# A kernel with sessions of matmuls on one core: small work between them spaced by sessions

## The chip, the cores and the metric

The kernel runs on one core of one Trainium2 chip. The metric is the time of one execution on the device in microseconds (us), first instruction to last with what lies around them; lower is better.

## What is computed

Agent attention for 4 batches, then a feed-forward layer with a squared ReLU on all 49920 tokens:

```python
def _attn_ref(q, k, v, agents):          # q, k, v: 4 x 12480 x 128; agents: 4 x 49 x 128
    scale = 1.0 / np.sqrt(q.shape[-1])
    def sm(a, b):
        s = scale * (a @ b.transpose(0, 2, 1))
        s = s - s.max(-1, keepdims=True)
        e = np.exp(s)
        return e / (e.sum(-1, keepdims=True) + 1e-09)
    agent_v = sm(agents, k) @ v          # 49 x 128 for each batch
    return sm(q, agents) @ agent_v

def _moe_ref(x, w_in, w_out):            # 128 -> 2048 -> 128
    h = np.maximum(x @ w_in, 0.0)
    return h * h @ w_out
```

The product of `agent_v` and `w_in` is formed once for each batch (the *table*, 49 x 2048), so a token needs its 49 softmax weights times the table (h), ReLU, square, and the product with `w_out`. Numbers are split into a high and a low part, so that products of short floats keep the precision of the long ones.

## The kernel before

Tokens go through in 52 *groups* of 960 (13 to a batch). A group has two halves of 480 tokens, a half has 8 *slots* of 256 hidden columns, and a half's slots go through in three *sessions* of 3, 3 and 2 slots (`SIZES`). A group's six sessions are called A1, A2, A3 (first half) and B1, B2, B3 here; A3 and B3 are the short ones. Session s does, in the loop at the end of the kernel:

- `first`: TensorE makes h of session s (`h<-w` with the weights w and the table's high part, then `h<-x` with the 19 rows of x that hold the rest), and ScalarE takes the ReLU (`r<-h`), slot by slot;
- `copied_out`: VectorE copies a finished half out of its PSUM bank (`ob<-o`; there is one such bank, `ps_o`);
- `squares`: ScalarE squares r (`r<-r`);
- `halved`: VectorE splits session s-1 into `g_hi` and `g_lo`;
- `second`: TensorE multiplies session s-2 by `w_out`: all `o<-g_hi`, then all `o<-g_lo` (LAG is 2).

On TensorE's queue a session is thus its h, then the products of the session two before it. Small work is put in between by Python generators, and one PSUM bank (`psa`, `ps_a` with bufs=1) takes all of its matmuls in turn: each must wait until the last one's result has been read.

- `queries` (named "ahead") makes one group's softmax weights, a group before they are used: the load of qt; its scores (`psa<-ag,qt`, 32 small matmuls); on VectorE m (maximum) and e; on ScalarE the exponential; on VectorE z, its reciprocal and `e<-e,z`; on ScalarE the cast to `pp`, on VectorE the low part `pp<-e,pp`; then for each half four transposes (`psa<-identr,pp`), ScalarE's `w<-psa` (w0, w1) and DMAs from w to w and to x. The transposes always stand behind the `o` products of B1 and B2 (a yield of "turn" marks them).
- `background(b)` (named "todo") makes the next batch's table: 13 blocks of keys (`psa<-ag,kt`, ScalarE's copy `s<-psa`, VectorE's `mx`), the maxima (`m1`, `dg`, `mb`), 13 blocks of values (`psa<-d,vt`, VectorE's `av`, then the next `d<-s,mb`), the sums (`rl`), and four products `psa<-win,avT`, each read by ScalarE's `aw_hi` and VectorE's `aw_lo`. It runs during three of the four batches; the last 13 groups have none.

A generator yields either nothing (its next step is taken by `between`, one for a slot, while "todo" is behind its goal) or a number of slots (its next step stands in `first`, at most one in a session, "ahead" before "todo"). What is issued through `queued` keeps this written order on its engine; other small instructions are placed by the scheduler, which models the engines. Weights w and x of half j are read by `h` of the next group's A1 (w0, x0) and B1 (w1, x1).

Of the kernel before, what the change touches and what calls it, by code (L numbers as in the profile page):

```python
# [17 lines left out]
P = 128  # L18
# [7 lines left out]
WIDEST = max(SIZES)  # L26
# [7 lines left out]
PRE = 10  # L34
RAW = 4
CT = 32
SPREAD = 0.88
BEGIN = 4
FIRST = 7

# [2 lines left out]
def agent_attention_relu2(ctx: ExitStack, tc: tile.TileContext, qT, kT, v, agT, w_in, w_out, outT):  # L43
    nc = tc.nc
    C, NTOK = qT.shape
    _, B, NA = agT.shape
    N = NTOK // B
    FF = w_in.shape[1]
# [3 lines left out]
    NK = len(blocks)  # L52
    K2 = 2 * NA
# [16 lines left out]
    class Ordered:  # L70
        def __init__(self, eng, always=False):
            self.eng, self.always = eng, always
# [6 lines left out]

    pe, act, dve, pool, sync = (Ordered(e) for e in (nc.tensor, nc.scalar, nc.vector, nc.gpsimd, nc.sync))  # L80

    fixed = Ordered(nc.scalar, True)

    def spare():
        return pool if alone[0] else dve
# [103 lines left out]
    def scores(b, i, kt):  # L189
        st = state.setdefault(b, {"s": []})  # L190
        _, rows, nt = blocks[i]
        yield 3
        sv = bank()[:rows, : nt * NA].rearrange("p (t a) -> p t a", a=NA)
        for t in range(nt):
            tiled(sv[:, t, :], kt[:, t * rows : (t + 1) * rows], ag[:, b, :])
        s = sp.tile([P, 512], F32, name="s")[:, : NT * NA].rearrange("p (t a) -> p t a", a=NA)
        st["s"].append(s)
        if i == 0:
            st["mx"] = small.tile([P, NT, NA], F32, name="mx")
        s, mx = (x[:rows, :nt, :] for x in (s, st["mx"]))  # L200
        fixed.copy(s, sv)
        if i == 0:
            dve.tensor_copy(mx, s)
        else:
            dve.tensor_max(mx, mx, s)

    def maxima(b):
        st = state[b]
        m1 = small.tile([P, NA], F32, name="m1")
        dve.reduce_max(m1, st["mx"].rearrange("p t a -> p a t"), axis=AX.X)  # L210
        yield
        pt = bank()
        pe.transpose(pt[:NA, :P], m1, ident)
        yield
        m2 = small.tile([NA, 1], F32, name="m2")
        dve.reduce_max(m2, pt[:NA, :P], axis=AX.X)
        dg = small.tile([NA, NA], F32, name="dg")
        dve.tensor_scalar_mul(dg, ident[:NA, :NA], m2)
        yield
        pb = bank()  # L220
        pe.matmul(pb[:, :NA], ones[:NA, :], dg, start=True, stop=True)
        yield
        st["mb"] = small.tile([P, NA], F32, name="mb")
        dve.tensor_copy(st["mb"], pb[:, :NA])

# [13 lines left out]
    def whole_sums(b):  # L239
        st = state[b]  # L240
        e1 = small.tile([P, 2, NA], F32, name="e1")
        dve.reduce_sum(e1[:, 0, :], st["mx"].rearrange("p t a -> p a t"), axis=AX.X)
        dve.tensor_copy(e1[:, 1, :], e1[:, 0, :])
        yield
        av = st["avT"] = small.tile([C, K2], F32, name="avT")
        dve.tensor_copy(av[:, :NA], st["av"])
        dve.tensor_copy(av[:, NA:], av[:, :NA])
        pz = bank()
        pe.matmul(pz[:K2, :1], e1.rearrange("p h a -> p (h a)"), ones[:, :1], start=True, stop=True)
        rl = st["rl"] = small.tile([K2, 1], F32, name="rl")  # L250
        dve.tensor_scalar_add(rl, pz[:K2, :1], 1e-9)
        dve.reciprocal(rl, rl)
# [20 lines left out]
    def tables(b):  # L273
        st = state[b]
        rl, av = st["rl"], st["avT"]
        hi = st["hi"] = aw.tile([P, FF], F32R, name="aw_hi")
        ex = st["lo"] = aw.tile([P, NCH // NQ, P], F32R, name="aw_ex")
        for n in range(FF // 512):
            yield
            cs = slice(n * 512, (n + 1) * 512)  # L280
            pw = bank()
            pe.matmul(pw[:K2, :], av, win[:, cs], start=True, stop=True)
            yield
            fixed.activation(hi[:K2, cs], pw[:K2, :], AF.Copy, scale=rl)
            lo = aw.tile([P, 512], F32R, name="aw_lo", bufs=3)[:NA, :]
            dve.scalar_tensor_tensor(  # L286
                out=lo, in0=pw[:NA, :], scalar=rl[:NA, :], in1=hi[:NA, cs].bitcast(F32),
                op0=ALU.mult, op1=ALU.subtract,
            )
            yield  # L290
            sync.dma_start(hi[K2:, cs].bitcast(F32), lo[:SP, :].bitcast(F32))
            for t in range(NQ):
                sync.dma_start(ex[t * 32 : t * 32 + NL, n, :].bitcast(F32), lo[SP:, t * P : (t + 1) * P].bitcast(F32))


    weights = {}
    slot = [0]

    def queries(g):
        b = g // NB  # L300
        qt = qp.tile([C, BLK], F32, name="qt", bufs=1)
        sync.dma_start(qt, qT[:, g * BLK : (g + 1) * BLK])
        yield 3
        ps = ps_a.tile([P, 512], F32, name="psa")
        sv = ps[:TP, : NT * NA].rearrange("p (t a) -> p t a", a=NA)
        for t in range(NT):
            tiled(sv[:, t, :], qt[:, t * TP : (t + 1) * TP], ag[:, b, :])
        if alone[0]:
            yield
        m = qp.tile([TP, NT, 1], F32, name="m", bufs=1)  # L310
        dve.reduce_max(m, sv, axis=AX.X)  # L311
        e = qp.tile([TP, NT, NA], F32, name="e", bufs=1)
        dve.tensor_sub(e, sv, m.broadcast_to([TP, NT, NA]))  # L313
        yield
        if not alone[0]:
            yield
        act.activation(e, e, AF.Exp, scale=scale)  # L317
        yield
        z = qp.tile([TP, NT, 1], F32, name="z", bufs=1)
        dve.reduce_sum(z, e, axis=AX.X)  # L320
        dve.tensor_scalar_add(z, z, 1e-9)
        dve.reciprocal(z, z)
        spare().tensor_mul(e, e, z.broadcast_to([TP, NT, NA]))  # L323
        yield
        pp = qp.tile([TP, NT, K2], F32R, name="pp", bufs=1)
        yield from halves(pp, e, NA, spare())
        weights[g] = []
        for j in range(2):
            yield "turn"
            pt = ps_a.tile([P, 512], F32, name="psa")  # L330
            for t in range(NT // 2):
                queued(
                    nc.tensor.matmul, nc.tensor, pt[:K2, t * TP : (t + 1) * TP], pp[:, j * (NT // 2) + t, :], identr, start=True, stop=True
                )
            w = qp.tile([P, G], F32R, name=f"w{j}", bufs=2)
            x = qp.tile([P, G], F32R, name=f"x{j}", bufs=2)
            fixed.copy(w[:K2, :], pt[:K2, :G])
            weights[g].append((w, x))
            yield
            sync.dma_start(w[K2:, :].bitcast(F32), w[:SP, :].bitcast(F32))  # L340
            for t in range(NQ):
                sync.dma_start(x[t * 32 : t * 32 + NL, :].bitcast(F32), w[SP:NA, :].bitcast(F32))
# [4 lines left out]
    SLOTS = 2 * NP  # L347
# [4 lines left out]
    def first(k, m):  # L352

        g, i = divmod(k, SLOTS)
        j, c = divmod(i, NP)
        b = g // NB
        w, x = weights[g][j]
        hs = [ps_h.tile([P, 2, 512], F32, name="h") for _ in range(m)]
        outs = [(2 * c + n, hs[n // 2][:, n % 2, :G]) for n in range(2 * m)]
        for n, out in outs:  # L360
            cs = slice(n * P, (n + 1) * P)
            queued(nc.tensor.matmul, nc.tensor, out, state[b]["hi"][:, cs], w, start=True, stop=False)

        with tc.high_priority():
            for n, out in outs:
                t = n % NQ
                rows = slice(t * 32, t * 32 + NL)
                queued(nc.tensor.matmul, nc.tensor, out, state[b]["lo"][rows, n // NQ, :], x[rows, :], start=False, stop=True)
        r = ffn.tile([P, WIDEST, 2, G], F32, name="r", bufs=RB)
        for x, h in enumerate(hs):  # L370
            queued(nc.scalar.activation, nc.scalar, r[:, x, :, :], h[:, :, :G], AF.Relu)
        for name in ("ahead", "todo"):
            if type(stands.get(name)) is int and k >= stands[name] and done[name] < goal[name]:
                move(name, k)
                break
        return r
# [65 lines left out]
        yield from whole_sums(b)  # L442
        yield from tables(b)

    STEPS = 2 + 2 * NK + 5 + 3 * NK + 1 + 3 * (FF // 512)

    def step(gen):

# [65 lines left out]
    turn = {}  # L514
# [179 lines left out]
    def between(k):  # L694
# [10 lines left out]
            following[0] = queries(g + 2)  # L705
            step(following[0])
        if c == 0 and 0 < g < B * NB - 1:
            gens["ahead"], stands["ahead"] = following[0], k + 1
        if stands["ahead"] is None and k > 0:
            move("ahead", k)  # L710

# [6 lines left out]
    made, split = {}, {}  # L718
    for s in range(len(sessions) + LAG):
        k, m = sessions[s] if s < len(sessions) else (total, 0)  # L720
        if s == LAG:
            behind = [chain[eng] for eng in (nc.tensor, nc.sync, nc.scalar, nc.vector, nc.gpsimd)]
        if m:
# [12 lines left out]
            halved(*sessions[s - 1], made.pop(s - 1), s <= LAG)  # L736
        if s >= LAG:
            second(*sessions[s - LAG])
            if stands.get("ahead") == "turn":
                move("ahead", slot[0])  # L740
        for x in range(1, m):
            between(k + x)
# [36 lines left out]
```

## Time and profile before

| | before |
|---|---|
| median of 3 runs (lowest to highest) | 2105.43 us (2100.71 to 2107.95) |
| the profiled execution: its time | 2101.62 us |
| its span, first to last instruction | 2099.6 us |
| mean granted TensorE clock | 0.969 |
| busy: TensorE, VectorE, ScalarE | 93 %, 78 %, 78 % |

In the profile PE is TensorE's matmuls, PEld its weight loads, DVE VectorE, ACT ScalarE, SP the queue of DMA issues. Nearly every row of PE, DVE and ACT carries line L64, the helper `queued`, so rows are told apart by their tiles (`o<-g_hi,wo_lo`). A timeline row gives the start, the duration, the engine, the operation and its tiles, how many alike were merged, and in brackets how long the engine had stood idle and who ended that.

### The profile page before, as it was taken

Reading aid. Unit: us, or ns where it says so; the run is one execution under the profiler, and the core shown is the slowest. Engines: PE = TensorE matmul, PEld = TensorE weight load, DVE = VectorE, ACT = ScalarE, POOL = GpSimd, SP = SyncE. Lnnn points to the kernel's source line nnn. Section 1 sums busy time; section 2 is a strip of 40 time slices with the busy share of each in tenths; the row PEclk is TensorE's granted clock in tenths of the full one; section 3 lists DMA queues with packets and bytes.
Section 4 is the critical chain, followed back from the end, with each engine's and each line's share of the span. In section 5 each row is a group of like instructions: output and inputs, shape, how many; then the busy total and the mean of one; then the engine's idle time right before and its main releaser. Section 6 shows DMA issues by size and latency. Waiting matters only on the chain.

```text
span 2099.6 us, 39766 instructions
## 1 busy us (share of the span) xinstructions
PE 1959.2 (93%) x17181; PEld 1508.9 (72%) x17181; DVE 1640.4 (78%) x1371; ACT 1637.7 (78%) x1516; POOL 20.6 (1%) x24
## 2 busy tenths in 40 slices
PE   7899999998999999998989999999899899989989
PEld 4677777776777777776767777777677677767767
DVE  7778888887778888887767888888677767767866
ACT  5788878887778888887777888888777777777876
POOL 3000000000000000000000000000000000000000
PEclk9999999999999999999999999999999999989989
DMA  9222222211112212211112212121111011001100
GB/s 359 75 83 73 67 73 78 67 53 40 39 62 78 87 59 80 82 59 36 43 41 77 82 52 82 60 70 45 32 40 42 27 37 39 32 30 36 42 20 25
DMA packets 54818, 131.46 MB, mean 63 GB/s; under 512 B 6508, under 2 KB 34828, under 8 KB 54644
## 3 DMA queue, kind: packets, MB, share of 16 engines
q1 hardware_dynamic: 54644, 128.93, 18.6%
q8 instruction: 135, 2.21, 0.4%
q14 instruction: 39, 0.32, 0.0%
HBM read 80.97 MB, written 25.56 MB: 51 GB/s over the span
## 4 chain that ended last, share of the span: by engine, by line
PE 55%; ACT 18%; DVE 17%; issue 9%; DMA 1%; SPq 0%; POOL 0%; ACTq 0%; DVEq 0%; POOLq 0%
PE o L64 32%; PE h L64 18%; ACT r L64 17%; DVE g_hi L64 7%; DVE g_lo L64 5%; PE psa L64 4%; DVE ob L64 1%; DVE pp L231 1%; DVE m L311 1%; DVE z L320 0%; DVE t L64 0%; DVE e L323 0%; DMA ahead<-in_kT 0%; DVE mx L64 0%; DMA x<-w 0%
## 5 line engine op out<-in xcount | busy, mean ns | idle before, releaser
L64 ACT ACTIVATE r<-h 128x960 f32<-128x960 f32 x832 | 752.0, 973 | 290.5 <-PE h L64 287.5
L64 DVE TENSOR_TENSOR g_lo<-r,g_hi 128x2880 fp32r<-128x2880 f32 (+2 forms) x315 | 880.4, 2796 | 15.0 <-PE psa L64 0.9
L64 ACT ACTIVATE r<-r 128x2880 f32<-128x2880 f32 (+2 forms) x315 | 733.0, 2328 | 7.7
L64 DVE CAST g_hi<-r 128x2880 fp32r<-128x2880 f32 (+2 forms) x315 | 464.9, 1476 | 291.8 <-ACT r L64 282.7
L64 PE MATMUL o<-g_hi,wo_lo 128*128 128x480 f32 x1664 | 682.5, 410 | 7.1 <-DVE ob L64 6.9
L64 PE MATMUL o<-g_hi,wo_hi 128*128 128x480 f32 x1664 | 647.6, 389 | 0.0
L64 PE MATMUL h<-w,aw_hi 128*128 128x480 f32 x1664 | 426.2, 387 | 0.4 <-DVE aw_hi L64 0.4
L64 PE MATMUL o<-g_lo,wo_hi 128*128 128x480 f32 x1664 | 426.2, 388 | 0.0
L64 PEld LDWEIGHTS o<-g_hi,wo_lo 128*128 128x128 f32 x1664 | 322.2, 194 | 117.3 <-issue 44.7
L64 PEld LDWEIGHTS o<-g_lo,wo_hi 128*128 128x128 f32 x1664 | 322.5, 194 | 52.6 <-issue 1.5
L64 PEld LDWEIGHTS o<-g_hi,wo_hi 128*128 128x128 f32 x1664 | 323.5, 194 | 42.1 <-issue 0.7
L64 PEld LDWEIGHTS h<-w,aw_hi 128*128 128x128 f32 x1664 | 305.6, 189 | 47.6 <-issue 2.0
L64 PE MATMUL h<-x,aw_ex 19*128 19x480 f32 x1664 | 204.4, 467 | 2.3 <-DMA x<-w 2.3
L64 PEld LDWEIGHTS h<-x,aw_ex 19*128 19x128 f32 x1664 | 84.8, 188 | 110.9 <-issue 107.9
L64 DVE COPY ob<-o 128x480 f32<-128x480 f32 x104 | 67.6, 650 | 84.7 <-PE o L64 84.3
L64 PE MATMUL psa<-identr,pp 120*98 120x120 f32 x416 | 54.9, 256 | 72.8 <-DVE pp L231 62.5
L64 PEld LDWEIGHTS psa<-identr,pp 120*98 120x98 f32 x416 | 50.8, 173 | 98.7 <-DVE pp L231 55.5
L64 ACT CAST w<-psa 98x480 fp32r<-98x480 f32 x104 | 57.2, 550 | 50.0 <-PE psa L64 50.0
L64 PE MATMUL psa<-ag,qt 128*32 128x49 f32 (+1 forms) x3328 | 48.4, 213 | 26.2 <-DVE aw_lo L286 21.7
L64 PEld LDWEIGHTS psa<-ag,qt 128*32 128x32 f32 (+1 forms) x3328 | 41.1, 111 | 43.2 <-DVE aw_lo L286 24.2
L231 DVE TENSOR_TENSOR pp<-e,pp 120x392 fp32r<-120x392 f32 x51 | 28.8, 564 | 21.0 <-ACT pp L229 21.0
L317 ACT ACTIVATE e<-e 120x392 f32<-120x392 f32 x51 | 26.7, 524 | 22.4 <-DVE e L313 22.2
(138 smaller groups left out, 624.4 us busy)
## 6 DMA issues: line engine op xcount, KB each, us to landing
qt<-in_qT SPq DMA_DIRECT2D x52, 480.0 KB
out_T<-ob SPq DMA_DIRECT2D x104, 240.0 KB
kt<-in_kT SPq DMA_DIRECT2D x36, 512.0 KB
vt<-in_v SPq DMA_DIRECT2D x36, 512.0 KB
x<-w SPq DMA_DIRECT2D x416, 35.6 KB
ahead<-in_kT SPq DMA_DIRECT2D x12, 512.0 KB
ahead<-in_v SPq DMA_DIRECT2D x12, 512.0 KB
w<-w SPq DMA_DIRECT2D x104, 56.2 KB
```

Source lines behind the costliest of these rows:

```text
L64: ins = issue(*args, **kw)
L231: eng.tensor_sub(out[:, :, n : n + w], x, out[:, :, :w].bitcast(F32))
L311: dve.reduce_max(m, sv, axis=AX.X)
L317: act.activation(e, e, AF.Exp, scale=scale)
```

## The change

- `queries`: its steps begin at slot 0 of a group and not at slot 1. A block of transposes waits for `Turn`: the first for two sessions after the step that made pp's low part, the second for the next session's end. While one is due, "todo" takes its step in `first` only in a session of full width (`due`).
- `scores`, `maxima`, `whole_sums`: other spacing, and the transposes and products of the maxima and sums go in their written place on TensorE (`put`).
- `tables`: the product and its two readers are issued in one step, two slots apart.
- `SPREAD` 0.88 becomes 0.98: the background's goal reaches the whole of its steps later in the batch; `STEPS` counts the fewer steps.

```diff
-SPREAD = 0.88
+SPREAD = 0.98
...
-    fixed = Ordered(nc.scalar, True)
+    fixed, put = Ordered(nc.scalar, True), Ordered(nc.tensor, True)
...
     def scores(b, i, kt):
-        yield 3
+        yield 2
...
         dve.reduce_max(m1, st["mx"].rearrange("p t a -> p a t"), axis=AX.X)
-        yield
+        yield 2
         pt = bank()
-        pe.transpose(pt[:NA, :P], m1, ident)
-        yield
+        put.transpose(pt[:NA, :P], m1, ident)
...
-        yield
+        yield 3
         pb = bank()
-        pe.matmul(pb[:, :NA], ones[:NA, :], dg, start=True, stop=True)
-        yield
+        put.matmul(pb[:, :NA], ones[:NA, :], dg, start=True, stop=True)
...
         for n in range(FF // 512):
-            yield
+            yield 2
             cs = slice(n * 512, (n + 1) * 512)
             pw = bank()
-            pe.matmul(pw[:K2, :], av, win[:, cs], start=True, stop=True)
-            yield
+            put.matmul(pw[:K2, :], av, win[:, cs], start=True, stop=True)
             fixed.activation(hi[:K2, cs], pw[:K2, :], AF.Copy, scale=rl)
...
+    class Turn:
+        def __init__(self, wait):
+            self.session = session[0] + wait
+
+    def due():
+        at = stands.get("ahead")
+        return isinstance(at, Turn) and session[0] >= at.session
...
         for j in range(2):
-            yield "turn"
+            yield Turn(0 if j or slot[0] < SLOTS else 2)
...
         for name in ("ahead", "todo"):
-            if type(stands.get(name)) is int and k >= stands[name] and done[name] < goal[name]:
+            if (m == WIDEST or not due()) and type(stands.get(name)) is int and k >= stands[name] and done[name] < goal[name]:
...
-    STEPS = 2 + 2 * NK + 5 + 3 * NK + 1 + 3 * (FF // 512)
+    STEPS = 2 + 2 * NK + 5 + 3 * NK + 1 + 2 * (FF // 512)
...
-            gens["ahead"], stands["ahead"] = following[0], k + 1
+            gens["ahead"], stands["ahead"] = following[0], k
...
             second(*sessions[s - LAG])
-            if stands.get("ahead") == "turn":
+            if due():
                 move("ahead", slot[0])
```

The change moves instructions on every engine. VectorE in a group of the last batch, before, from z in A2 to the split of B1 (`r` is what ScalarE squared; 2880 is a session of three slots, 1920 of two):

```order
L320 TENSOR_REDUCE z<-e 120x8
L64 TENSOR_TENSOR g_lo<-r,g_hi 128x2880
L321 TENSOR_SCALAR z<-z 120x8
L64 CAST g_hi<-r 128x1920
L322 RECIPROCAL z<-z 120x8
L64 TENSOR_TENSOR g_lo<-r,g_hi 128x1920
L323 TENSOR_TENSOR e<-e,z 120x392
L64 CAST g_hi<-r 128x2880
L231 TENSOR_TENSOR pp<-e,pp 120x8x49
L64 TENSOR_TENSOR g_lo<-r,g_hi 128x2880
```

The same engine and work in the changed kernel, from the end of B3 of the group before to the split of A2:

```order
L319 TENSOR_TENSOR e<-psa,m 120x392
L64 CAST g_hi<-r 128x2880
L326 TENSOR_REDUCE z<-e 120x8
L64 TENSOR_TENSOR g_lo<-r,g_hi 128x2880
L327 TENSOR_SCALAR z<-z 120x8
L64 COPY ob<-o 128x480
L328 RECIPROCAL z<-z 120x8
L329 TENSOR_TENSOR e<-e,z 120x392
L64 CAST g_hi<-r 128x2880
L229 TENSOR_TENSOR pp<-e,pp 120x8x49
L64 TENSOR_TENSOR g_lo<-r,g_hi 128x2880
```

The low part of pp, which the transposes behind the products of B1 read, stood between the halves of the split of B1; now it stands in that of A2, two sessions earlier, and z has moved in front of `ob`, where m stood.

VectorE in the same place of a group with blocks of values behind it, in the changed kernel (A1):

```order
L64 CAST g_hi<-r 128x2880
L326 TENSOR_REDUCE z<-e 120x8
L64 TENSOR_TENSOR g_lo<-r,g_hi 128x2880
L327 TENSOR_SCALAR z<-z 120x8
L268 TENSOR_TENSOR av<-av,psa 128x49
L235 TENSOR_TENSOR d<-s,mb 128x392
L328 RECIPROCAL z<-z 120x8
L329 TENSOR_TENSOR e<-e,z 120x392
L64 COPY ob<-o 128x480
```

Here four small operations stand between `z<-z` and `ob` that stand behind it, or elsewhere, in the other groups.

ScalarE at the last product of a table, before:

```order
L64 ACTIVATE r<-h 128x960 x3
L64 ACTIVATE r<-r 128x2880
L64 ACTIVATE aw_hi<-psa,rl 98x512
L317 ACTIVATE e<-e 120x392
L229 CAST pp<-e 120x8x49
```

and in the changed kernel, at the last two:

```order
L64 ACTIVATE r<-h 128x960 x3
L64 ACTIVATE aw_hi<-psa,rl 98x512
L64 ACTIVATE r<-r 128x2880
L227 CAST pp<-e 120x8x49
L64 ACTIVATE r<-h 128x960 x2
L64 ACTIVATE aw_hi<-psa,rl 98x512
L64 ACTIVATE r<-r 128x1920
```

`aw_hi`, which reads the product out of the bank, has moved in front of the squares of the session that issues the product; before, it stood behind the squares of the session after it.

## Rows read from the trace of the kernel before

**Rows 1.** The page, part 1: busy us, share, instructions of each engine.

```profile
PE 1959.2 (93%) x17181; PEld 1508.9 (72%) x17181; DVE 1640.4 (78%) x1371; ACT 1637.7 (78%) x1516; POOL 20.6 (1%) x24
```

**Rows 2.** Waits of PE: who waited for whom, total us, times, longest us.

```profile
PE psa L64 <- DVE pp L231: 62.5, 32, 3.3
PE psa L64 <- DVE aw_lo L286: 21.7, 6, 6.6
PE psa L64 <- DVE av L270: 9.4, 12, 1.1
PE o L64 <- DVE ob L64: 6.9, 24, 0.6
```

**Rows 3.** Timeline of PE, last batch: the transposes behind B1's products.

```profile
1597.70 0.56 PE L64 MATMUL psa<-identr,pp 120*98 120x120 f32 x4 [3.27 <-DVE pp L231]
```

**Rows 4.** Windows: length; busy of PE, PEld, DVE, ACT, POOL; PEclk; DMA share, GB/s.

```profile
1010.92:1045.19 34.27, 33.98 (x233) 26.63 (x232) 26.82 (x18) 29.23 (x25) 0.00 (x0) 1.00 0.13 42
1010.92:1017.26 6.34, 6.34 (x36) 5.03 (x34) 3.45 (x3) 4.38 (x4) 0.00 (x0) 1.00 0.00 0
1017.26:1022.37 5.11, 5.11 (x31) 3.94 (x30) 4.04 (x2) 4.48 (x6) 0.00 (x0) 1.00 0.08 20
1588.19:1598.09 9.90, 6.63 (x35) 4.94 (x34) 7.98 (x9) 6.26 (x6) 0.00 (x0) 1.00 0.00 0
1598.09:1606.26 8.17, 8.17 (x30) 6.01 (x30) 2.81 (x2) 5.86 (x5) 0.00 (x0) 0.58 0.07 21
345.63:352.84 7.21, 6.57 (x36) 4.94 (x34) 6.11 (x10) 4.82 (x6) 0.00 (x0) 1.00 0.00 0
352.84:359.76 6.92, 6.21 (x95) 4.65 (x94) 5.39 (x5) 6.73 (x6) 0.00 (x0) 1.00 0.14 39
810.64:848.85 38.21, 36.94 (x425) 28.81 (x424) 32.28 (x31) 31.51 (x29) 0.00 (x0) 1.00 0.24 79
1536.00:1541.59 5.59, 5.59 (x90) 4.36 (x88) 4.22 (x2) 4.86 (x5) 0.00 (x0) 1.00 0.27 78
1492.92:1507.60 14.68, 8.12 (x89) 6.42 (x88) 8.64 (x10) 8.32 (x8) 0.00 (x0) 0.65 0.13 36
```

**Rows 5.** Timeline, last batch, A1 to A3: end of h, the split, ob, pp.

```profile
1572.25 0.70 PE L64 MATMUL h<-x,aw_ex 19*128 19x480 f32 x6
...
1578.17 1.66 DVE L64 CAST g_hi<-r 128x2880 fp32r<-128x2880 f32 x1 [4.11 <-ACT r L64]
...
1583.48 0.65 DVE L64 COPY ob<-o 128x480 f32<-128x480 f32 x1
...
1584.18 0.48 PE L64 MATMUL o<-g_hi,wo_lo 128*128 128x480 f32 x1 [0.24 <-DVE ob L64]
...
1597.08 0.56 DVE L231 TENSOR_TENSOR pp<-e,pp 120x392 fp32r<-120x392 f32 x1
```

**Rows 6.** Timeline of PE at the end of a batch: the table's last products.

```profile
1486.36 1.10 PE L282 MATMUL psa<-win,avT 128*98 128x512 f32 x2 [1.56 <-DVE aw_lo L286]
...
1501.59 1.53 PE L64 MATMUL psa<-ag,qt 128*32 128x49 f32 x64 [6.56 <-DVE aw_lo L286]
```

**Rows 7.** Timeline of PE: a block of values in B3, behind w1's transposes.

```profile
398.93 0.91 PE L64 MATMUL psa<-d,vt 128*32 128x49 f32 x64 [1.20 <-ACT w L64]
```

**Rows 8.** Groups of DVE by form: busy us, mean ns of one, idle before.

```profile
L237 DVE TENSOR_TENSOR d<-s,mb 128x392 f32<-128x392 f32 x33 | 18.2, 559 | 0.0
...
L270 DVE TENSOR_TENSOR av<-av,psa 128x49 f32<-128x49 f32 x36 | 7.2, 200 | 0.0
```

**Rows 9.** Timeline: w0's cast and the next h that reads x0, twice.

```profile
91.25 0.54 ACT L64 CAST w<-psa 98x480 fp32r<-98x480 f32 x1
...
102.01 0.77 PE L64 MATMUL h<-x,aw_ex 19*128 19x480 f32 x3 [1.45 <-DMA x<-w]
...
1018.10 0.54 ACT L64 CAST w<-psa 98x480 fp32r<-98x480 f32 x1
...
1029.21 0.71 PE L64 MATMUL h<-x,aw_ex 19*128 19x480 f32 x6
```

More of the change, by code (lines that the diff above doesn't have):

```diff
@@ L248, in whole_sums @@
         pz = bank()
-        pe.matmul(pz[:K2, :1], e1.rearrange("p h a -> p (h a)"), ones[:, :1], start=True, stop=True)
+        put.matmul(pz[:K2, :1], e1.rearrange("p h a -> p (h a)"), ones[:, :1], start=True, stop=True)
         rl = st["rl"] = small.tile([K2, 1], F32, name="rl")
@@ L278, in tables @@
         for n in range(FF // 512):
-            yield
+            yield 2
             cs = slice(n * 512, (n + 1) * 512)
             pw = bank()
-            pe.matmul(pw[:K2, :], av, win[:, cs], start=True, stop=True)
-            yield
+            put.matmul(pw[:K2, :], av, win[:, cs], start=True, stop=True)
             fixed.activation(hi[:K2, cs], pw[:K2, :], AF.Copy, scale=rl)
@@ L293, in tables @@
                 sync.dma_start(ex[t * 32 : t * 32 + NL, n, :].bitcast(F32), lo[SP:, t * P : (t + 1) * P].bitcast(F32))
+    class Turn:
[4 more added lines that the diff above has]
+        return isinstance(at, Turn) and session[0] >= at.session
+    session = [0]
     weights = {}
@@ L720, in agent_attention_relu2 @@
         k, m = sessions[s] if s < len(sessions) else (total, 0)
+        session[0] = s
         if s == LAG:
```

## The prediction

> **What bounds the kernel now.** First the busy shares: TensorE is busy 93 % of the span, VectorE and ScalarE 78 % each [rows 1], so TensorE's queue sets the end, and what can be won is its idle time (140 us: the span less its busy time) and the time in which its clock is low. Then the waits of TensorE: 62.5 us of idle time end with VectorE's low part of pp, 21.7 us with `aw_lo`, 9.4 us with `av` [rows 2]. A timeline shows where the first stands: the transposes behind the products of B1 find pp unfinished for 3.27 us [rows 3]. Then windows, cut at the first `h<-w` of each session. Two groups without background work differ only in that wait: one without it takes 34.27 us; in one with it B1 takes 9.90 us where 6.34 are enough, and B2 8.17 us at a granted clock of 0.58 where 5.11 are enough at 1.00 [rows 4]. So a wait of 3.3 us costs 3.56 us at once, and 3.06 us more because the clock was at its lower level, 1.2 GHz, for most of the session after it. In the trace 17 groups have such a wait (two of 2.8 us, fifteen of 3.3): the 13 of the last batch, and 4 where the background has run out or begins. In 13 of them B2 is as slow as in the row; in one it loses 1.4 us, in three nothing.
>
> **What the change does, priced.** The edits go by what they move.
>
> *Scores a session earlier, pp out of B1.* TensorE's work is the same: the score matmuls move from A2 to A1, and the transposes stay behind B1 and B2. VectorE's `pp` moves from the split of B1 to that of A2, two sessions of TensorE ahead of its readers. So the wait for pp goes with all that it costs: 15 x 3.56 + 2 x 3.0 + 13 x 3.06 + 1.4 = 100.6 us. In the 12 groups with blocks of values the wait is short, and B1 takes 7.21 us in place of 6.34 [rows 4]: 0.8 us on the mean of the 12, 9.8 in all. Together -110 us. What hides pp from now on is the two sessions; if VectorE fell that far behind, the wait would be back.
>
> *A table's readers with its product.* Before, the last `aw_hi` stood behind the squares of the next session; the scores waited 6.56 us for its `aw_lo` [rows 6], and the session took 14.68 us at clock 0.65 where 5.59 are enough [rows 4]: 9.1 us, three times, 27.3. The product before waits 1.56 us [rows 6] and one more 0.7 (the six waits of 21.7 us less the three long ones [rows 2]), three times each: 6.8. Now `aw_hi` follows the ReLU of its own session at once and delays the squares by its 0.7 us, which the two sessions between h and its products cover. What is left is the second product, in B2: its `aw_lo` stands behind the split of B1, and the transposes that need the bank come after a short session's products. By the nearest place, the wait for `av` below, 1.3 us, three times: 3.9. Net -30 us.
>
> *Blocks of values, two in a group and not three.* Where a block stands in B2, the transposes behind it wait for `av`: B2 takes 6.92 us [rows 4], and 5.11 with 0.85 for the block would be 5.96. That happens 12 times [rows 2]; six such places stay: -6 us.
>
> *New or longer waits.* (1) The products that follow h of A3 open a new half and need the bank that `ob` empties. In the last batch A1's h ends at 1572.95, its split begins at 1578.17, `ob` starts at 1583.48, and those products wait 0.24 us for it [rows 5]. There m stood in front of `ob`; now z stands there and is as long: 17 groups stay as they are, +0.1 us each. But in 12 groups with values `av`, d, a reciprocal and `e<-e,z` stand in front: 0.20 and 0.56 us [rows 8], and by the like sizes 0.20 and 0.56, together 1.5 us, against which TensorE has one block (0.85 us) more in A2. So 0.9 us each, the old 0.24 included: 11 us. Three groups with a short block 0.6 each, three with the maxima `m1` 1.5 each. In groups with keys a block in A3 stands ahead of the products and covers it. Sum +19 us. (2) A block in B3 needs the bank that w1's cast empties, and the cast stands behind the squares of B2. The trace has that wait, 1.20 us [rows 7], once or twice in a batch. The order now has such a place 12 times (six blocks of keys, six of values): 12 x 1.2 = 14.4 us, less 6.7 for like places that go: +8 us. (3) A copy `mb` behind B1's split, in front of the transposes of B2, 1.2 us three times, against two like waits that go: -1 us.
>
> *SPREAD and the fewer steps* only move blocks: as many matmuls, over more groups. The last product of a table stands in A3 of a batch's last group, four sessions before its first reader, and that covers its DMAs. The wait for x0 in the second group [rows 9] stays: TensorE gets there some 2 us sooner and waits for the same DMA; 0, between -2 and +2.
>
> Sum: -110 - 30 - 6 + 19 + 8 - 1 = -120 us. Against the profiled execution's own 2101.6 us that is 1982 us, **the prediction**. That execution is 3.8 us under the median of the runs, 2105.4, so measured by the median the gain would be a little larger.
>
> **The clock, and a rule against this change.** What stays is many short waits in place of few long ones. First the row: a group with five waits of 0.5 to 0.7 us, 38.21 us in all, ran at 1.00 throughout [rows 4]; so short waits are priced at their length. The Trainium skill, TensorE: Matmul & The Clock Gate, section "A second HAM failure mode: psum-queue depth-cycling", tells of a kernel whose TensorE often idled briefly between groups of matmuls, while it cycled through PSUM banks, and whose clock swung between its two levels for that. By that rule rival A would hold; this case's row disagrees.
>
> **Rivals.**
>
> A. *Short waits lower the clock.* About 39 waits of 0.6 us or more stay by my count (15 + 12 + 6 + 6); if each made the next session as slow as the slow B2, 39 x 3.06 = 119 us would come back: 2101 us, no change. Against it: the row at 1.00. For it: in the changed kernel nearly every group with background work has two or three of them.
>
> B. *VectorE becomes the bound.* With the waits gone TensorE's groups are 6.6 us shorter, and VectorE has to do the same in less time. For it: the operations ahead of `ob`. Against it: in a clean group VectorE is busy 26.82 of 34.27 us [rows 4]. If the waits that stay are twice as long as priced (I count some 50 us of them behind the second group), 2032 us.
>
> C. *x0 arrives too late* (slower). w0's cast cannot move forward with pp: it stands behind B1's squares. In the second group the last piece of x came 10.2 us after the end of the cast (91.79, 102.01) [rows 9], and TensorE waited; in a clean group the h that reads x0 begins 10.6 us after it (1018.64, 1029.21) [rows 9], without a wait. In the groups with a slow B2 that distance was 3 us longer; now all groups run without, and more blocks share the DMA engines. If x0 came 3.3 us too late in all 51 groups that have one, each would lose 3.56 us at once, 182 in all, and up to 3.06 more for the clock: 2164 to 2320 us. It turns slower than before from 120 / 51 = 2.4 us of wait in each group on. Against it: the clean groups show no such wait, and a block in B2, B3 or A1 lengthens the distance by 0.85 us. The Trainium skill, DMA: Bandwidth & Descriptors, section "Anatomy of one DMA — SWDGE (gpsimd) path", fits about 2 us of fixed time to one DMA (on GpSimd's path); two in a row would land well before the read, and this rival would fall. The row is far longer, so I keep it.
>
> **Numbers.** About 0.3 % (6 us) is what a measurement of this kernel can tell from no change. The forecast, the long waits gone and short ones left at their length, has 0.80 and its own bounds: 1945 (most of the new short waits don't appear, -36) and 2018 (they are two thirds longer than priced). B beyond 2018 has 0.06, A 0.05 (no change), C 0.05 (slower), and 0.04 is for less than 1945, where waits that I leave in place go as well. So faster 0.90, same 0.05, slower 0.05; the range 1945 to 2018 leaves out 0.2.
>
> **What would show it.** Right: no wait of TensorE for pp over 0.3 us; PEclk 1.00 from the third group to the end; groups of the last batch 34.3 to 34.5 us each; waits for `aw_lo` under 5 us in all; `ob` and `w` at the head of TensorE's waits with some 25 and 15 us. Wrong: a PEclk under 0.95 in groups without a long wait (A); `o<-g_hi` or `o<-g_lo` waiting for the split (B); `h<-x` waiting for the DMA of x in most groups (C); or the transposes still waiting for pp, two sessions then being too few.

## The result, and the profile after

The changed kernel takes 1960.49 us (median of 4 runs, 1959.76 to 1961.24), the kernel before in the same comparison 2104.78 us: a ratio of 0.9315, 95% interval 0.9299 to 0.9332, 144 us less. The profiled execution took 1959.76 us (span 1957.7), 142 us less than that of before; 120 were forecast against it.

The page of the changed kernel, part 1 and the granted clock of part 2:

```profile
PE 1902.4 (97%) x17181; PEld 1479.6 (76%) x17181; DVE 1641.2 (84%) x1371; ACT 1628.1 (83%) x1516; POOL 20.7 (1%) x24
...
PEclk9999999999999999999999999999999999999999
```

Beside [rows 1]: TensorE's busy time is 57 us shorter with as many instructions, because almost nothing runs at the lower clock any more (mean 0.996, before 0.969): from the third group to the end every session is at 0.99 or 1.00. Its idle time went from 140 to 55 us. VectorE and ScalarE do the same work in a shorter span.

The waits of TensorE, changed kernel (who waited for whom, total us, times, longest us):

```profile
PE o L64 <- DVE ob L64: 16.7, 33, 1.4
PE psa L64 <- ACT w L64: 11.8, 12, 1.2
...
PE psa L64 <- DVE aw_lo L283: 2.3, 3, 0.8
PE h L64 <- DMA x<-w: 2.3, 3, 1.0
PE psa L64 <- DVE mb L222: 2.1, 3, 0.7
PE psa L64 <- DVE av L268: 1.4, 6, 0.3
```

Against [rows 2]: no wait for pp is left, those for `aw_lo` and `av` shrank from 21.7 and 9.4 us to 2.3 and 1.4, and `ob` and `w` stand in front.

Windows of the changed kernel: a group of the last batch, its B1 and B2, a group with values, and an A3 of the last batch (columns as in [rows 4]):

```profile
1639.98:1674.20 34.22, 34.07 (x233) 26.64 (x232) 29.42 (x22) 30.06 (x27) 0.00 (x0) 1.00 0.12 42
1657.23:1663.62 6.39, 6.39 (x35) 5.02 (x34) 5.37 (x3) 5.28 (x5) 0.00 (x0) 1.00 0.00 0
1663.62:1668.76 5.14, 5.14 (x30) 3.95 (x30) 4.09 (x2) 4.47 (x6) 0.00 (x0) 1.00 0.06 16
1247.05:1283.83 36.78, 35.90 (x361) 28.09 (x360) 31.22 (x29) 31.43 (x29) 0.00 (x0) 1.00 0.24 78
1651.59:1657.23 5.64, 5.49 (x27) 4.26 (x26) 5.29 (x8) 5.61 (x5) 0.00 (x0) 1.00 0.11 44
```

B1 and B2 are within 0.05 us of the 6.34 and 5.11 us that the clean group of [rows 4] had, where 9.90 and 8.17 stood.

One session still runs low, A1 of the second group: there TensorE waits for x0 three times (0.57, 0.99 and 0.71 us), and the clock is at 0.74. Before, it waited twice in that place (0.89 and 1.45 us), at 0.71.

```profile
96.92:109.89 12.97, 10.70 (x97) 7.84 (x96) 5.77 (x6) 6.39 (x6) 0.00 (x0) 0.74 0.21 63
```

Timeline of the changed kernel, last batch: pp's low part, the first transposes, w0's cast, the next h that reads x0.

```profile
1621.60 0.56 DVE L229 TENSOR_TENSOR pp<-e,pp 120x392 fp32r<-120x392 f32 x1
...
1629.12 0.48 PE L64 MATMUL psa<-identr,pp 120*98 120x120 f32 x4
...
1630.29 0.53 ACT L64 CAST w<-psa 98x480 fp32r<-98x480 f32 x1
...
1641.39 0.71 PE L64 MATMUL h<-x,aw_ex 19*128 19x480 f32 x6
```

In [rows 3] the transposes waited 3.27 us for pp; here pp ended 7.0 us ahead of them. x0 is read 10.6 us after the cast's end, as before [rows 9], without a wait.

And the two waits that now lead, in two neighbouring groups with values: a block in B3 behind w1's cast, and the products of A3 behind `ob`, which stands behind four small operations.

```profile
1242.16 0.91 PE L64 MATMUL psa<-d,vt 128*32 128x49 f32 x64 [1.17 <-ACT w L64]
...
1259.47 0.17 DVE L327 TENSOR_SCALAR z<-z 120x8 f32<-120x8 f32 x1
1259.54 0.20 DVE L268 TENSOR_TENSOR av<-av,psa 128x49 f32<-128x49 f32 x1
1259.66 0.56 DVE L235 TENSOR_TENSOR d<-s,mb 128x392 f32<-128x392 f32 x1
...
1260.37 0.57 DVE L329 TENSOR_TENSOR e<-e,z 120x392 f32<-120x392 f32 x1
1260.85 0.65 DVE L64 COPY ob<-o 128x480 f32<-128x480 f32 x1
...
1261.56 0.49 PE L64 MATMUL o<-g_hi,wo_lo 128*128 128x480 f32 x1 [0.63 <-DVE ob L64]
```

### The profile page after: what moved, and what is told of

It reads as the page before. It is cut to its first block, busy times and chain, and to the rows that moved or that the text cites. A ratio compares the mean times of both kernels' runs of the same rounds, so it can differ in the third digit from the quotient of the medians.

```text
span 1957.7 us, 39753 instructions
## 1 busy us (share of the span) xinstructions
PE 1902.4 (97%) x17181; PEld 1479.6 (76%) x17181; DVE 1641.2 (84%) x1371; ACT 1628.1 (83%) x1516; POOL 20.7 (1%) x24
## 4 chain that ended last, share of the span: by engine, by line
PE 65%; ACT 16%; DVE 11%; issue 7%; DMA 1%; SPq 0%; ACTq 0%; DVEq 0%
PE o L64 40%; PE h L64 19%; ACT r L64 15%; PE psa L64 5%; DVE g_hi L64 4%; DVE g_lo L64 4%; DVE ob L64 1%; DMA ahead<-in_kT 0%; DVE t L64 0%; DVE mx L64 0%; ACT w L64 0%; DMA x<-w 0%; DVE d L235 0%; DVE rest L64 0%; DVE z L327 0%
## 5 line engine op out<-in xcount | busy, mean ns | idle before, releaser
L64 PE MATMUL o<-g_hi,wo_lo 128*128 128x480 f32 x1664 | 669.2, 402 | 17.4 <-DVE ob L64 16.7
L64 PE MATMUL o<-g_hi,wo_hi 128*128 128x480 f32 x1664 | 632.6, 380 | 0.0
L64 PE MATMUL h<-w,aw_hi 128*128 128x480 f32 x1664 | 419.5, 383 | 0.4 <-DVE aw_hi L64 0.4
L64 PE MATMUL o<-g_lo,wo_hi 128*128 128x480 f32 x1664 | 413.0, 380 | 0.0
L64 PEld LDWEIGHTS o<-g_hi,wo_lo 128*128 128x128 f32 x1664 | 313.6, 188 | 118.1 <-DVE ob L64 32.9
L64 PEld LDWEIGHTS o<-g_lo,wo_hi 128*128 128x128 f32 x1664 | 313.9, 189 | 48.9
L64 PEld LDWEIGHTS o<-g_hi,wo_hi 128*128 128x128 f32 x1664 | 314.1, 189 | 42.3 <-issue 2.9
L64 PE MATMUL h<-x,aw_ex 19*128 19x480 f32 x1664 | 198.8, 455 | 2.3 <-DMA x<-w 2.3
L64 PEld LDWEIGHTS psa<-ag,kt 128*32 128x32 f32 x2340 | 28.2, 110 | 16.6 <-ACT w L64 6.5
L64 PEld LDWEIGHTS psa<-d,vt 128*32 128x32 f32 (+1 forms) x2160 | 26.4, 109 | 19.0 <-ACT w L64 8.9
```

Source lines behind the costliest of these rows:

```text
L64: ins = issue(*args, **kw)
```

## The experiments

All medians in one table first; the ratio is to the kernel before on the same chip, with its 95% interval.

| kernel | median us | ratio |
|---|---|---|
| tables' part alone | 2131.88 | 1.0132 (1.0117 to 1.0147) |
| scores' part alone | 2023.16 | 0.9616 (0.9600 to 0.9632) |
| scores' and tables' parts | 1980.21 | 0.9413 (0.9397 to 0.9428) |
| the change without the scores' part | 2163.79 | 1.0287 (1.0262 to 1.0313) |
| the change with SPREAD 0.88 | 1958.17 | 0.9305 (0.9291 to 0.9319) |
| the change, transposes behind B2 and B3 | 2254.40 | 1.0713 (1.0695 to 1.0730) |
| the change, `ob` copied three times | 2095.33 | 0.9953 (0.9934 to 0.9971) |
| the change, `ob` copied five times | 2210.30 | 1.0509 (1.0494 to 1.0525) |
| the change, one session's distance | 1949.06 | 0.9263 (0.9249 to 0.9277) |
| that, `ob` ahead inside the split | 1934.50 | 0.9200 (0.9186 to 0.9213) |
| that, the sum behind the split | 1934.22 | 0.9193 (0.9179 to 0.9207) |
| one session's distance, `ob` ahead, uncut | 1929.88 | 0.9172 (0.9160 to 0.9185) |

### 1. Scores back in A2, transposes a session later

```diff
-            gens["ahead"], stands["ahead"] = following[0], k
+            gens["ahead"], stands["ahead"] = following[0], k + 1
...
-            yield Turn(0 if j or slot[0] < SLOTS else 2)
+            yield Turn(0 if j or slot[0] < SLOTS else 1)
```

> The changed kernel with the scores back in A2 and the first transposes one session behind the step that makes pp's low part, so that they stand behind B1 and B2 as ever; tables, spacing and SPREAD stay changed. Theory (the gain is mostly the wait for pp and the clock that goes with it): TensorE waits for pp again, about 3.3 us in B1 in some 17 groups and about 0.6 us in the groups with values, B2 in the groups of the last batch runs at about 0.58 again, and of the 113 us that the places of pp gave some 100 come back: 2060 us, between 2045 and 2080. Rival (the gain comes from where the blocks and the table's readers stand): under 1990 us, with few waits for pp.

Measured: 2254.40 us, outside both. The edit does not do what the expectation says: with the step of pp one session later and one session's distance, the transposes stand behind B2 and B3, not B1 and B2. So it measured rival C instead. Waits of TensorE, and a timeline of w0's cast and the next `h<-x` in a group of the last batch:

```profile
PE h L64 <- DMA x<-w: 123.7, 144, 1.2
```

```profile
1912.09 0.54 ACT L64 CAST w<-psa 98x480 fp32r<-98x480 f32 x1
...
1918.79 0.48 PE L64 MATMUL h<-x,aw_ex 19*128 19x480 f32 x1 [0.56 <-DMA x<-w]
1920.37 0.52 PE L64 MATMUL h<-x,aw_ex 19*128 19x480 f32 x1 [1.10 <-DMA x<-w]
1921.78 0.77 PE L64 MATMUL h<-x,aw_ex 19*128 19x480 f32 x3 [0.89 <-DMA x<-w]
```

The last quarter of x0 is there 9.2 us after the cast's end. In the changed kernel the first read comes 10.6 us after it: by this, an estimate, x0 has some 1.4 us to spare. A cast one session later costs 294 us in 51 groups, 5.8 us in each, inside the range that rival C had (2164 to 2320 us).

Only 121 of the 294 us are the waits for x; 168 are TensorE's busy time, which grew from 1902.4 us with the same instructions. So the clock was low, though none of these waits is longer than 1.2 us. Part 1 of the page, and the A1 whose reads are shown above:

```profile
PE 2070.0 (92%) x17181; PEld 1583.4 (70%) x17181; DVE 1645.7 (73%) x1371; ACT 1636.7 (73%) x1516; POOL 20.7 (1%) x24
```

```profile
1916.31:1928.80 12.49, 9.95 (x33) 7.12 (x33) 5.04 (x4) 5.97 (x5) 0.00 (x0) 0.73 0.08 26
```

This A1 waits 0.56, 1.10 and 0.89 us and is busy 9.95 us; the shortest A1 of this make-up takes 6.02. In all 44 groups whose A1 has three or four such waits its clock is 0.73 to 0.87. Several short waits in one session thus lower the clock as one long wait does.

### 2. The scores' part alone

```diff
+    def due():
+        at = stands.get("ahead")
+        return isinstance(at, Turn) and session[0] >= at.session
...
-            yield "turn"
+            yield Turn(0 if j or slot[0] < SLOTS else 2)
...
-            gens["ahead"], stands["ahead"] = following[0], k + 1
+            gens["ahead"], stands["ahead"] = following[0], k
```

> The kernel before with the scores in A1 and the transposes two sessions behind pp's low part; nothing else of the change. Theory: the 113 us of the places of pp come as a gain, some 9 us of waits for ob are added; but the scores now stand right behind a table's product in A1 whose aw_hi still stands behind the squares of that session, twice in a batch: six waits of 5 to 7 us where there were three, 20 to 30 us more with the clock. About 2025 us, between 2000 and 2045: less than the whole of the term for pp, because that part leans on the part of the tables. Rival (the parts do not touch): 2000 us or less, with three waits for aw_lo.

Measured: 2023.16 us, as expected. Waits of TensorE:

```profile
PE psa L64 <- ACT w L64: 24.8, 21, 1.2
...
PE psa L64 <- DVE aw_lo L286: 16.7, 3, 5.6
```

No wait for pp is left, but three waits of some 5.6 us for `aw_lo` are, as many as the rival had, where I had counted six. In the other three of the six sessions in which scores follow a table's product, the next h waits 1.6 us for ScalarE's ReLU. The six together are 36.5 us longer than they need be, so the time is the theory's. 21 waits of blocks for w1's cast are left as well.

### 3. The tables' part alone

```diff
-            yield
+            yield 2
             cs = slice(n * 512, (n + 1) * 512)
             pw = bank()
-            pe.matmul(pw[:K2, :], av, win[:, cs], start=True, stop=True)
-            yield
+            put.matmul(pw[:K2, :], av, win[:, cs], start=True, stop=True)
...
-    STEPS = 2 + 2 * NK + 5 + 3 * NK + 1 + 3 * (FF // 512)
+    STEPS = 2 + 2 * NK + 5 + 3 * NK + 1 + 2 * (FF // 512)
```

> The kernel before with only the tables' part: product and readers in one step, two slots apart, in the written place. Theory: the three waits of 6.6 us for aw_lo and the 1.6 us waits ahead of them go, nothing else: 31 us less, 2074 us, between 2066 and 2085; the waits for pp stay at about 62 us. Rival (the readers ahead of the squares delay ScalarE, and so the split, and the waits come back elsewhere): 2090 us or more.

Measured: 2131.88 us, 28 us slower than before where I expected 31 less. Waits of TensorE, and its timeline behind B1 in the group at the end of the first batch:

```profile
PE psa L64 <- DVE pp L231: 90.5, 39, 3.4
```

```profile
518.89 0.56 PE L64 MATMUL psa<-identr,pp 120*98 120x120 f32 x4 [3.27 <-DVE pp L231]
```

The waits for `aw_lo` went, as expected, down to one of 0.3 us. But the waits for pp rose from 62.5 us [rows 2] to 90.5, the long ones from 17 to 26. In that group TensorE stood 6.56 us for `aw_lo` in A2 before, and its transposes behind B1 found pp ready; with A2's wait gone they wait 3.27 us for pp, and B2 is slow. There the one wait had covered the other: while TensorE stood, VectorE caught up.

### 4. One session's distance

```diff
-            yield Turn(0 if j or slot[0] < SLOTS else 2)
+            yield Turn(0 if j or slot[0] < SLOTS else 1)
```

> The changed kernel with one session between the step that makes pp's low part and the first transposes, not two: the transposes stand behind the products of A3 and B1, so w0's cast comes a session sooner. Theory (the wait goes because pp is ready; two sessions are more than it takes): in a group of the last batch pp ends at 16.3 us behind the start of A1's h and the products of A3 end at about 17, so no wait for pp over 0.3 us; the blocks in B3 no longer wait for w1's cast, 10 to 14 us less: 1950 us, between 1942 and 1962. Rival (two sessions are needed): waits for pp of 0.5 us and more in most groups, 1980 us or more.

Measured: 1949.06 us, as expected, and no wait for pp or for w is left. The first row of the waits is

```profile
PE o L64 <- DVE ob L64: 24.3, 56, 1.4
```

So two sessions are one more than pp needs. With one, w1's cast comes behind the squares of B1, and no block waits for it: 11.4 us less than the changed kernel.

### 5. The wait for pp, put back

```diff
-            gens["ahead"], stands["ahead"] = following[0], k
+            gens["ahead"], stands["ahead"] = following[0], k + 1
...
-            yield Turn(0 if j or slot[0] < SLOTS else 2)
+            yield Turn(0 if j or slot[0] < SLOTS else 0)
```

> The changed kernel with the scores back in A2, pp's low part in the split of B1 and the transposes behind B1 and B2, as before the change; tables, spacing and SPREAD stay changed. (In the first experiment the transposes had moved a session later, behind B2 and B3, so that one priced a late x0 and not the wait for pp.) Theory, as the tables alone suggest: the wait for pp is not tied to 17 groups; it stands wherever nothing earlier in the group has held TensorE, so with the tables' waits gone it is in more groups than before, some 25 long ones of 3.3 us and their slow B2: 2125 us, between 2095 and 2150. Rival (only the 113 us of the places of before come back): 2060 to 2085.

Measured: 2163.79 us, over the range. Waits of TensorE:

```profile
PE psa L64 <- DVE pp L229: 103.4, 35, 4.1
```

32 of these waits are longer than 2 us, in 32 of the 51 groups, and behind 27 the next session runs at a low clock. Among them are most groups with values, where before the wait was 0.6 us. So the scores' part is worth 203 us to the changed kernel, and the rest of the change without it costs 60 us.

### 6 and 7. Longer waits, to see the clock

`ob` is copied again, the same values, in front of A3's products:

```diff
-            queued(nc.vector.tensor_copy, nc.vector, ob, o[:, :G])
+            for _ in range(3 if t % BLK else 1):
+                queued(nc.vector.tensor_copy, nc.vector, ob, o[:, :G])
```

(5 in place of 3 in the second.)

> The changed kernel with ob copied three times in place of once where it empties the bank for A3's products (the same values): TensorE's wait there grows by about 1.7 us in each of 51 groups. Theory (a wait of this size is paid at its length, the clock stays at 1.00): 51 x 1.7 = 87 us more, 2047 us, between 2025 and 2065, granted clock 0.99 or more. Rival A (many short waits lower the clock): some 3 us more for each, 2150 us or more, clock under 0.97.

> The same with four copies more: waits of about 3.0 us in 51 groups. Theory (a wait of about 3 us lowers the clock of the session behind it, as the wait for pp did in 13 of 17 places): 51 x 3.0 = 153 us at once and some 3 us in most groups for the clock, 2235 us, between 2190 and 2270, granted clock about 0.93. Rival (the slow B2 came of something else in that place): 2113 us at a clock of 0.99.

Measured: 2095.33 us (ten runs, 2082.80 to 2099.64, granted clock 0.965 to 0.974) and 2210.30 us (clock 0.947). The second time is in the theory's range; the first lies between the theory's range and the rival's, at a clock near the rival's. Waits, and the window of an A3 with a wait of 1.89 us, with two copies more:

```profile
PE o L64 <- DVE ob L64: 97.6, 53, 3.1
```

```profile
1760.20:1769.04 8.84, 6.95 (x27) 5.45 (x26) 8.81 (x11) 6.36 (x5) 0.00 (x0) 0.81 0.07 28
```

and with four copies more, the waits and an A3 with a wait of 3.27 us:

```profile
PE o L64 <- DVE ob L64: 176.1, 53, 4.5
```

```profile
1853.83:1865.07 11.24, 7.97 (x27) 6.27 (x26) 10.87 (x13) 6.35 (x5) 0.00 (x0) 0.70 0.06 22
```

The waits for `ob` grew by 81 us with two copies, TensorE's busy time by 58 (1960.4 us, the same instructions); with four copies by 159 and 90 (1992.9 us). The busy time is the clock: the A3 with 1.89 us of wait is 8.84 us long, against 5.64 with 0.15; 1.74 us of that is wait, 1.46 the clock. In the A3 with 3.27 us the clock costs 2.48 (7.97 us busy, against 5.49). Sorted by the length of the wait, the A3 sessions whose mean granted clock is under 0.95:

| wait for `ob`, us | changed kernel | two copies more | four copies more |
|---|---|---|---|
| 0.55 to 0.93 | 0 of 13 | 0 of 6 | |
| 1.28 to 1.47 | 0 of 3 | 2 of 9 | |
| 1.86 to 2.02 | | 15 of 18 | |
| 2.22 to 2.68 | | 13 of 15 | 5 of 7 |
| 2.75 to 4.52 | | 3 of 3 | 41 of 44 |

The first row and the last are as priced, but for the clock's own cost: 1.8 us on the mean of 51 groups with four copies more, where some 3 were expected in most. That a wait of 1.9 us is among the dear ones I had not expected.

### 8. `ob` ahead of the small operations

With one session's distance. VectorE's split of A1 and B1 does two of its three slots, copies `ob`, and goes on; z's small steps behind its sum (the addition of 1e-9, the reciprocal, the product with e), av and d follow `ob`. The sum itself (`z<-e`) stays ahead of the low part.

```diff
+        for x in [slice(0, m - 1), slice(m - 1, m)] if between_them else pieces(m, apart):
             queued(nc.vector.tensor_sub, nc.vector, lo[:, x, :, :], r[:, x, :, :], hi[:, x, :, :].bitcast(F32))
+            if between_them:
+                between_them()
+                between_them = None
...
-            dve.tensor_add(st["av"], st["av"], pv[:C, :NA])
+            later(lambda: dve.tensor_add(st["av"], st["av"], pv[:C, :NA]))
```

> The kernel of one session's distance, with the split's low part that runs ahead of ob cut at two of its three slots, ob copied there, and z's sum, its reciprocal, the product with z, av and d behind ob. Theory: the waits for ob, 24 us in 56 places with one session's distance, are all that is left in the groups; they go to under 4 us: 1949 less 20 is 1929 us, between 1922 and 1938. Rival (TensorE then waits for the split, which ends 0.7 us later with the copy inside it, or for pp): 1945 us or more.

Measured: 1934.50 us, in the theory's range, 15 us under one session's distance where 20 were expected. The waits for `ob` are gone, and one for pp has taken the place of part of them; the timeline shows VectorE idle ahead of `ob` in a group with values:

```profile
PE psa L64 <- DVE pp L229: 9.5, 16, 0.9
```

```profile
366.69 2.15 DVE L64 TENSOR_TENSOR g_lo<-r,g_hi 128x1920 fp32r<-128x1920 f32 x1
369.95 0.66 DVE L64 COPY ob<-o 128x480 f32<-128x480 f32 x1 [1.12 <-PE o L64]
```

### 9. Scores' and tables' parts together

The edits of 2 and 3 in one kernel.

> The kernel before with the scores' part and the tables' part together, without the other spacing (steps of scores and maxima) and with SPREAD 0.88. Theory (each part needs the other: the scores' part alone left six long waits behind a table's product, 36.5 us; the tables' part alone uncovered more waits for pp): the 36.5 us go to some 3, nothing new comes: 2023 less 33 is 1990 us, between 1978 and 2003. What is left to the changed kernel, some 30 us, is then the spacing: 21 waits for w1's cast in B3, and the maxima. Rival (the parts add up as they measured alone, 81 less and 28 more): 2050 us.

Measured: 1980.21 us, 10 less than the theory's figure and inside its range. Neither the long waits for `aw_lo` nor those for pp are there:

```profile
PE psa L64 <- ACT w L64: 21.2, 18, 1.2
PE o L64 <- DVE ob L64: 18.1, 39, 1.2
...
PE psa L221 <- DVE dg L218: 5.1, 3, 2.2
```

Alone, the parts gave 81 us less and 28 more; together they give 123 less. Behind the scores' part the tables' part is worth 43 us; ahead of it, it costs 28.

### 10. SPREAD

```diff
-SPREAD = 0.98
+SPREAD = 0.88
```

> The changed kernel with SPREAD 0.88. Theory (it only moves blocks; three more blocks of values stand in B3 and wait 1.2 us for w1's cast, three less in B2): 1962 us, between 1956 and 1969, no difference that counts. Rival (the wider spread keeps VectorE from falling behind in the groups with values): 1975 us or more.

Measured: 1958.17 us. 2.3 us less than the changed kernel is under the 6 us that count here: SPREAD is worth nothing by itself here, as expected. So, by difference, the 20 us between 9 and the changed kernel are the other spacing and the written places of scores, maxima and sums: the waits for w1's cast are 11.8 us and not 21.2, and the three for dg are gone.

### 11. The sum behind the split

```diff
-            spare().tensor_add(es, es, e)
+            summed_later.append(lambda: dve.tensor_add(es, es, e))
```

> The kernel with ob ahead, and in the groups with values the sum of the exponentials (mx<-mx,d) behind the split and not ahead of pp's low part. Theory: the 16 waits for pp that are left, 9.5 us, go to under 3: 1934 less 6 is 1928 us, between 1923 and 1933. Rival (the sum delays the next split by as much): 1934 us again.

Measured: 1934.22 us: the rival, no change (17 waits for pp, 9.7 us). The sum now stood ahead of the next split, and pp began where it had.

### 12. `ob` ahead, uncut

The low part of the split stays whole, `ob` follows it at once, all small operations of the groups follow `ob`, and pp's low part has a written place between the halves of A2's split.

```diff
             second(*sessions[s - LAG])
+            if ends:
+                copied_out()
             if due():
                 move("ahead", slot[0])
...
+        while in_split:
+            queued(*in_split.pop(0))
         for x in pieces(m, apart):
             queued(nc.vector.tensor_sub, nc.vector, lo[:, x, :, :], r[:, x, :, :], hi[:, x, :, :].bitcast(F32))
...
-            dve.tensor_max(mx, mx, s)
+            later(nc.vector.tensor_max, mx, mx, s)
```

> One session's distance; ob directly behind the whole low part of the split (not cut: with the cut VectorE stood 1.1 us idle in the groups with values, until TensorE's half was done), all small operations of the groups behind ob, and pp's low part in its written place between the halves of A2's split. Theory: the 9.5 us of waits for pp that the two runs before had left go, because pp comes 1.1 us sooner, and ob comes no later than with the cut: 1934 less 9 is 1925 us, between 1919 and 1931. Rival (ob behind the whole split is late again, or pp's fixed place holds up the split): 1934 us or more.

Measured: 1929.88 us, in the theory's range and 31 us under the changed kernel; of all kernels here the fastest. Waits, and VectorE in a group with values:

```profile
PE o L64 <- DVE ob L64: 5.5, 17, 1.2
```

```profile
1229.42 3.15 DVE L64 TENSOR_TENSOR g_lo<-r,g_hi 128x2880 fp32r<-128x2880 f32 x1
1232.68 0.66 DVE L64 COPY ob<-o 128x480 f32<-128x480 f32 x1
1233.26 0.16 DVE L64 TENSOR_SCALAR z<-z 120x8 f32<-120x8 f32 x1
...
1236.75 0.57 DVE L64 TENSOR_TENSOR pp<-e,pp 120x392 fp32r<-120x392 f32 x1
```

`ob` no longer stands behind four operations, and no wait for pp is left.

## Why the prediction was right, and where it was not

The sum was compared term by term in this way: the length of every session from the fifth on, less the shortest of its make-up (slots, block, transposes), added up by what the session holds. Before, some 200 us stood over the shortest; now some 57.

| term | forecast us | measured us |
|---|---|---|
| wait for pp, with its clock (B1, B2) | -110 | -113.0 |
| table's readers | -30 | -31.4 |
| values in B2, wait for `av` | -6 | -10.1 |
| `ob` ahead of A3's products | +19 | +9.2 |
| blocks in B3, wait for w1's cast, less like places that go | +8 | +4.5 |
| maxima (`mb`) | -1 | -1.4 |
| sum | -120 | -142.2 |

- **pp: right**, in place, in size and in what the clock gives back. The signs named for it came: no wait for pp, clock at 0.99 or 1.00 from the third group on, last-batch groups of 34.1 to 34.5 us (34.3 to 34.5 were named), 2.3 us of waits for `aw_lo`, `ob` and `w` at the head (with 16.7 and 11.8 us, under the 25 and 15 named).
- **What was mis-sized are the new short waits**, the step "Sum +19 us" above all: `ob` was priced at 0.9 us in the 12 groups with values by adding up the four operations in front of it, and measured 0.55 to 0.63; and the 0.24 us of the last batch, which I raised by 0.1, came out at 0.15 (the A3 above: 5.64 us, 5.49 of them busy). Next, the six blocks of values that stay in B2 wait 0.2 to 0.3 us and cost 0.5, not 1.0, and four of six blocks of keys in B3 wait 0.6 us and not 1.2. These three erred to the same side and make 17 of the 22 us between the sum and what was measured; the range (1945 to 2018) holds it.
- **The terms are not each edit's own worth**, though the text reads so. "Net -30" for the tables and "-6" for the blocks hold only once pp is out of B1. Alone, the tables' part costs 28 us (experiment 3), and all the rest without the scores' part costs 60 (experiment 5): with other waits of TensorE gone, the long waits for pp are in more groups, 17 before, then 26, then 32, and experiment 3 shows for one group how the first wait had covered the second. The sum came out right because the wait that the others would have uncovered was taken away in the same change.
- **Rival A (short waits lower the clock)** did not come, but less spoke against it than the text has it. The row at 1.00, 38.21 us with 36.94 of them busy [rows 4], has two waits, one in each of two sessions, and not five. The waits of TensorE in that stretch, before:

```profile
PE psa L64 <- DVE av L270: 0.7, 1, 0.7
PE psa L64 <- DVE pp L231: 0.6, 1, 0.6
```

In the changed kernel, too, no session from the third group on has more than one wait, none is longer than 1.41 us, and none ran low. Whether the waits stand one to a session the prediction did not weigh, and it matters: three in one session, each of 1.2 us or less, lower the clock in the second group and in nearly all groups of experiment 1. Single waits of 1.9 us do in 15 of 18 places (experiment 6). The Trainium skill, TensorE: Matmul & The Clock Gate, section "A second HAM failure mode: psum-queue depth-cycling", tells of a clock that swings because TensorE idles briefly and often. The changed kernel's waits, some 60 of them at a clock of 0.996, do not bear that out; the A1 sessions of experiment 1 agree with it.

- **Rival B**: VectorE went from 78 % to 84 % and set no wait beyond those listed.
- **Rival C** did not hold: x0 is still in time in all groups but the second, by the estimate with about 1.4 us to spare. Its price held the time of experiment 1, which missed by one session and paid 294 us, but for other amounts: 2.4 us of waits in a group and not 3.56, and 3.3 us for the clock, which the text had as at most 3.06. The Trainium skill, DMA: Bandwidth & Descriptors, section "Anatomy of one DMA — SWDGE (gpsimd) path", has about 2 us of fixed time for one DMA on GpSimd's path. No run here shows that path; on SP's queue the last of the five DMAs behind a cast was there 9.2 us after it (experiment 1), so the rival was rightly kept.
- **SPREAD at 0: right** (experiment 10).

What is argued and not shown: why the waits for pp in experiment 5 come in just those 32 groups. Two blocks of values to a group, not three, let TensorE reach B1's transposes sooner, and experiment 3 shows that less delay ahead of them brings the wait; no run takes out single blocks.

## What to carry to other kernels

Price an edit that removes a wait together with what the waiting engine meets next: an engine that stands still lets the others catch up, so a wait taken away alone can come back at once in another place (28 us slower here), and two such edits can be worth far more together than apart. Move the late producer first, then remove the waits that had covered it. Where a short wait is left, look at what small work stands in front of the operation that ends it: putting `ob` ahead of four small operations, with one session's distance, took 31 us more.

## What the runs showed of the hardware

Single waits of TensorE for `ob`, of 0.55 to 1.41 us, left the granted clock at 1.00 in all 16 places of the changed kernel; of 1.28 to 1.47 us lowered it in 2 of 9 sessions, of 1.86 to 2.02 us in 15 of 18, of 2.75 us and more in 44 of 47. Short waits close together did the same: three or four waits for x in one session, each of 1.2 us or less, lowered it in all 44 such sessions of experiment 1. What a low clock costs depends on the place: 1.5 us for the rest of an A3 behind a wait of 1.9 us and 2.5 behind one of 3.3, with the next session at 1.00 again; 3.06 us in B2 behind the waits of 3.3 us for pp [rows 4]. Why it lasts longer there, and why some waits of the same length leave the clock at 1.00, no run here tells.
